# A third chunk projected from rows turned with both LayerNorm factors, a third pair of turned-row buffers, and a new order for the MLP and its two ends

## The chip, the cores and the metric

The kernel runs on one core of one Trainium2 chip. Its time is in device microseconds (us) for one execution; runs of the kernel before lie between 1086.4 and 1087.1 us.

## The reference, cut to what matters

One sequence of 2048 rows `x` with 448 columns, all float32. `xn` is the LayerNorm of `x`; the result is `x + attention(xn) + mlp(layernorm(xn))`.

```python
xn = layernorm(x)
# A: 16 query heads of 28, one shared key head and one shared value head
q = (xn @ wq) split into 16 heads; k = xn @ wk; v = xn @ wv
A = softmax(q k^T / sqrt(28)) v, heads joined, @ wo
# B: a second LayerNorm, then two dense layers (448 -> 1792 -> 448)
y = layernorm(xn)
B = gelu(y @ w1 + b1) @ w2 + b2
out = x + A + B
```

The second LayerNorm of an already normalised row differs from the first by one factor for each row. So every row has a first factor `lnr` (for the projections) and the product of both, `lnq` (for the MLP).

## The kernel before, in words

The rows are handled in four chunks, 0 to 3, of 512 rows (four tiles of 128). There are three stages, laid out in one program order by Python code; each engine works its own instructions strictly in that order.

**Projections (about 0 to 65 us).** For chunk c there are four `q_slot`s (c, 0) to (c, 3), each of eleven matmuls on TensorE (PE) that project the chunk on 128 of 512 columns of wk, wv and wq; a factor of float32 precision is got from a high and a low part (`xh`, `xl`; `wah`, `wal`). While chunk c is projected, chunk c+1 is made ready (`norm_parts`, L273): `center` (L280) scales and shifts a tile on ScalarE (ACT, 448 columns, L288) and its last 64 columns once more on VectorE (DVE, L289); `turn` (L293) turns it by four PE transposes (L297), and ACT (L298) and DVE (L299) write it to `xh` and `xl`. The statistics of a chunk are DVE chains (`bn`, `bn_end`, `rstd`: L194 to L240) with one square root on ACT. The result of a q_slot is evacuated by `evac` (L385) during the next slot: ACT writes the high part (L389) and DVE the low part (L396), which leave by DMA. At (c, 0) ACT also writes `vt`, which PE turns (L410) two slots on and DVE copies (L411).

A chunk in `KEPT` (L35: 2 and 3) is turned once only, with `lnq`, and its turned rows stay for the MLP. Its projections need `lnr`: `unscale` (L248) spreads the ratio of the factors over the partitions with four float32 matmuls (L251) and an ACT copy `ib`, and every evac of this chunk starts with a DVE multiplication by `ib` (L388). A chunk that isn't kept (0 and 1) is turned a second time, with `lnq`, during the MLP. The dictionary `more`, filled by `later`, holds jobs (statistics, second factors, unscale) for the slot in which they are put in.

**MLP (about 65 to 471 us).** 56 slots n, one for each chunk in `MLP_ORDER` (2, 3, 0, 1) and each of 14 blocks ft of 128 hidden columns. Slot n holds the first layer of its block (`mlp1`, L636: eleven matmuls into the PSUM tile `ph`, then the GELU by ACT and GpSimd (POOL), in pieces `middle` and `ending`), and the second layer of the block of slot n-2 (`mlp2`, L662: twelve matmuls L673 from `hh`, `hl` and the weights `w2h`, `w2l`). The weights of the second layer are split by `w2_split` (L362: ACT `high` L367, then DVE and POOL `low` L371) for two blocks at a time. The dictionary `stages` of `slot` (L683) says after which of the twelve matmuls a piece is issued. Between these matmuls stand steps of two streams of the attention: `mxs` (scores whose maxima DVE takes, L561 and L562) and `tq` (scores of the heads that are turned by way of DRAM, L595, with DVE L596, ACT L613 and four DMAs). Their PSUM tiles `m` share three banks here.

**Attention (about 471 to 1085 us).** Scores L931, exponentials L932, the weighted sum L903, with the rest of `mxs` and `tq` between; what is left of `mxs` is shared out over the steps. Loads of this stage are issued from POOL (`loads = pool`, L949).

Of the kernel before, what the change touches and what calls it, by code (L numbers as in the profile page):

```python
# [16 lines left out]
P = 128  # L17
# [17 lines left out]
KEPT = 2, 3  # L35
MLP_ORDER = 2, 3, 0, 1
# [5 lines left out]
def block_kernel(ctx, tc, x, wq, wk, wv, wo, w1, b1, w2, b2, out):  # L42
# [11 lines left out]
    xt_p = ctx.enter_context(tc.tile_pool(name="xt", bufs=2))  # L54
# [18 lines left out]
    xl_p = ph1.enter_context(tc.tile_pool(name="xl", bufs=2))  # L73
# [120 lines left out]
    def rstd(dst, var, n, norms):  # L194
        m = len(norms)
        v = tmp.tile([P, 3, m, n], F32, name=f"rs{m}{n}", bufs=2)
# [20 lines left out]
    def bn_end(c, k0=0, n=CT):  # L217
# [10 lines left out]
        if c in KEPT:  # L228
            ratio = ratios[c] = tmp.tile([P, CT], F32, name="ratio", bufs=2)
            dve.tensor_mul(ratio, at[:, 1], lnq[:, ts])  # L230
# [42 lines left out]
    def norm_parts(c, second, first=False, bank=mtile):  # L273
        second = second or c in KEPT
# [5 lines left out]
        def center(k):  # L280
# [3 lines left out]
            else:  # L284
                xn = tmp.tile([P, 4 * P], F32, name="xn", bufs=2)
# [3 lines left out]
            dve.tensor_scalar(xn[:, D:512], src[:, 384:448], scale[:, t:t + 1], bias[:, t:t + 1],  # L289
                              op0=ALU.mult, op1=ALU.add)  # L290
# [12 lines left out]
    def norm_first(bank):  # L303
        center, turn = norm_parts(0, False, True, bank)
        ends = seconds
# [122 lines left out]
    seconds = [bn_end(0, 0, 2), bn_end(0, 2, 2)]  # L428
    norm_first(qbank)
    seconds.append(stats(1))  # L430
# [5 lines left out]
    for c, at in ((2, ((0, 1), (0, 2), (0, 2), (0, 3))), (3, ((1, 0), (1, 1), (1, 2), (1, 3)))):  # L436
# [6 lines left out]
        later(c - 1 if c == 2 else c, 3 if c == 2 else 0, lambda c=c: unscale(c), c == 3)  # L443
    for g, at in zip((seconds[0], seconds[1], seconds[2]), ((2, 2), (2, 2), (1, 0))):
        later(*at, lambda g=g: next(g))
    for g in seconds[0:2]:
        later(2, 3, lambda g=g: next(g))
    later(2, 3, lambda: act.activation(warm, one, AF.Tanh))
# [28 lines left out]
    for c in range(NCH):  # L477
        if c + 1 < NCH:
            center, turn = norm_parts(c + 1, False, bank=lambda shape: (qbank, mtile)[next(turns) % 2](shape))
        for i in range(4):  # L480
# [23 lines left out]
            for part, k in (("", "c0 c1", "t0 c2 t1 c3", "t2 t3") if c == 0 else  # L504
# [131 lines left out]
    def mlp1(c, ft):  # L636
# [5 lines left out]
        hz = hrp.tile([P, CW], F32, name="hz", bufs=2)  # L642
        act.activation(hx, ph, AF.Identity, bias=b1t[:, ft:ft + 1])  # L643
# [18 lines left out]
    def mlp2(c, ft, stages):  # L662
# [20 lines left out]
    def slot(n):  # L683
# [330 lines left out]
```

## Time and profile before

| | |
|---|---|
| median of 3 runs | 1086.64 us (1086.4 to 1087.1) |
| profiled execution | 1086.84 us |
| its span | 1085.1 us |
| granted TensorE clock | 0.999 |
| PE busy | 1072.9 us |
| DVE busy | 907.4 us |
| ACT busy | 726.8 us |
| POOL busy | 562.0 us |

The span is the time from the first to the last instruction of the profiled execution. A busy PE does not mean a PE at its peak: matmuls are pipelined and each record is longer than the distance to the next one, so what a step costs on PE is read from the distance between the starts of records. In a timeline a row has its start, its length, the engine, the line, the operation and the tiles; a bracket gives how long the engine sat idle before it and what ended that.

### The profile page before, as it was taken

To read this page: it belongs to the slowest core of one execution; us is meant where nothing else is said; L and a number is where in the kernel's file an instruction comes from. 1 tells how busy PE (TensorE), PEld (TensorE's weight loads), DVE (VectorE), ACT (ScalarE), POOL (GpSimd) and SP (SyncE) were. 2 spreads that over 40 slices of the span, in tenths; PEclk is the share of its full clock that TensorE was granted. 3 is DMA by queue.
4 is the path that set the end of the run, shared out by engine and by line. 5 is a ranking of instruction groups with operands and counts; after the bars stand their busy time and mean duration, and the time that the engine had idled before them with its cause. 6 is when DMAs were issued, how large, how long until landed. Compare 5 with 4: busy or idle time off the path is not lost.

```text
span 1085.1 us, 17677 instructions
## 1 busy us (share of the span) xinstructions
PE 1072.9 (99%) x5889; PEld 721.6 (67%) x5889; DVE 907.4 (84%) x1846; ACT 726.8 (67%) x1262; POOL 562.0 (52%) x694
## 2 busy tenths in 40 slices
PE   9989999999999999999999999999999999999998
PEld 8768888888888888865555556555556555555455
DVE  6789899898988998877999997899997889886744
ACT  6665556666666666559777776677775777765784
POOL 5359897778777877854333433433442343243220
PEclk9999999999999999999999999999999999999999
DMA  8774456777877777776977798588796778885820
GB/s 268 251 213 140 121 142 170 195 179 179 214 187 180 184 196 192 210 163 152 201 187 185 179 219 206 145 196 190 184 212 172 177 174 199 201 200 131 186 53 34
DMA packets 140102, 194.45 MB, mean 179 GB/s; under 512 B 17078, under 2 KB 95596, under 8 KB 140012
## 3 DMA queue, kind: packets, MB, share of 16 engines
q1 hardware_dynamic: 127276, 171.43, 62.8%
q0 software_dynamic: 11328, 21.33, 8.5%
q8 instruction: 46, 0.75, 0.3%
q10 hardware_dynamic: 1408, 0.57, 0.2%
q14 instruction: 44, 0.36, 0.1%
HBM read 114.30 MB, written 77.71 MB: 177 GB/s over the span
## 4 chain that ended last, share of the span: by engine, by line
PE 90%; DMA 4%; DVE 3%; issue 1%; POOL 1%; ACT 1%; SPq 0%; DVEq 0%; POOLq 0%; ACTq 0%
PE po L903 21%; PE m L561 18%; PE m L931 17%; PE m L673 12%; PE ph L182 10%; PE m L595 5%; DMA raw<-in_B_w_dram 1%; PE m L793 1%; PE m L794 1%; PE m L795 1%; PE ph L185 1%; PE ph L187 1%; PE po L886 1%; PE m L886 1%; DMA a<-in_A_x_dram 1%
## 5 line engine op out<-in xcount | busy, mean ns | idle before, releaser
L562 DVE TENSOR_REDUCE mx<-m 128x1 f32<-128x512 f32 x784 | 506.5, 679 | 78.2 <-PE m L561 68.4
L932 ACT ACTIVATE p<-m 128x512 f32<-128x512 f32 x784 | 402.6, 609 | 161.4 <-PE m L931 161.2
L561 PE MATMUL m<-ks,qm 128*128 128x512 f32 x784 | 321.4, 410 | 0.7 <-DVE mx L562 0.6
L931 PE MATMUL m<-xh,ks 128*128 128x512 f32 x784 | 257.3, 397 | 0.1
L903 PE MATMUL po<-p,vs 128*32 128x512 f32 x1920 | 230.8, 598 | 0.0
L561 PEld LDWEIGHTS m<-ks,qm 128*128 128x128 f32 x784 | 147.0, 187 | 116.8 <-ACT p L932 37.0
L596 DVE TENSOR_SCALAR_CACHE_REDUCE raw<-m 128x512 f32<-128x512 f32 x240 | 161.6, 689 | 17.4 <-PE m L595 10.6
L931 PEld LDWEIGHTS m<-xh,ks 128*128 128x128 f32 x784 | 146.1, 188 | 42.1 <-issue 5.8
L914 DVE STREAM_TRANSPOSE p<-half 128x1024 f32<-128x1024 f32 x120 | 148.2, 1236 | 5.3 <-PE m L886 2.0
L613 ACT ACTIVATE raw<-raw,m 128x1024 f32<-128x1024 f32 x120 | 133.0, 1150 | 2.0 <-DVE m L602 2.0
L903 PEld LDWEIGHTS po<-p,vs 128*32 128x32 f32 x1920 | 50.1, 109 | 113.4 <-issue 108.4
L643 ACT ACTIVATE hx<-ph,b1t 128x512 f32<-128x512 f32 x55 | 37.9, 690 | 124.2 <-PE ph L187 120.2
L595 PE MATMUL m<-ks,q 128*128 128x512 f32 x240 | 94.6, 394 | 1.7 <-DVE raw L596 1.7
L658 POOL TENSOR_TENSOR hl<-hx,hh 128x512 fp32r<-128x512 f32 x56 | 72.5, 1295 | 33.2 <-ACT hh L656 33.2
L673 PE MATMUL m<-w2h,hl 128*128 128x448 f32 x224 | 82.1, 368 | 1.4 <-POOL hl L658 1.4
L673 PE MATMUL m<-w2l,hh 128*128 128x448 f32 x224 | 81.4, 365 | 0.6 <-DVE w2l L371 0.6
L673 PE MATMUL m<-w2h,hh 128*128 128x448 f32 x224 | 81.3, 364 | 0.2 <-DMA td<-raw 0.2
L646 POOL TENSOR_TENSOR hz<-hz,hx 128x512 f32<-128x512 f32 x56 | 72.8, 1300 | 4.7
L548 POOL DMA_DIRECT2D xh<-mn x15 | 8.2, 545 | 129.2 <-ACT mn L544 129.2
L651 POOL TENSOR_TENSOR hx<-hx,hz 128x512 f32<-128x512 f32 x56 | 72.4, 1293 | 4.7
L182 PE MATMUL ph<-xh,w1h 128*128 128x512 f32 x165 | 65.0, 394 | 0.0
L182 PE MATMUL ph<-xh,w1l 128*128 128x512 f32 x165 | 64.5, 391 | 0.0
(182 smaller groups left out, 1384.0 us busy)
## 6 DMA issues: line engine op xcount, KB each, us to landing
td<-raw SPq DMA_DIRECT2D x240, 256.0 KB
half<-td SPq DMA_DIRECT2D x120, 512.0 KB
xh<-qd POOLq DMA_DIRECT2D x60, 168.0 KB, 4.2
a<-in_A_x_dram SPq DMA_DIRECT2D x28, 224.0 KB
qm<-qd POOLq DMA_DIRECT2D x112, 56.0 KB, 4.2
qd<-qe SPq DMA_DIRECT2D x24, 256.0 KB
qm<-qd SPq DMA_DIRECT2D x84, 56.0 KB
ad<-a SPq DMA_DIRECT2D x16, 224.0 KB
```

What stands on the lines that cost most here:

```text
L182: pe.matmul(ps, w, v, start=(n == 0), stop=False)
L561: pe.matmul(pm, qm[:, t * P:(t + 1) * P], ks[:, n * CW:(n + 1) * CW], start=True, stop=True)
L562: dve.tensor_reduce(mx[:, CT * j + t, n:n + 1], pm, axis=AX.X, op=ALU.max)
L595: pe.matmul(sc, q3[i][:, t * P:(t + 1) * P], ks[:, n * CW:(n + 1) * CW], start=True, stop=True)
L596: dve.tensor_scalar(raw[:, :, 4 * n:4 * n + 4, :].rearrange("p r b i -> p b r i"), sc.rearrange("p (b r i) -> p b r i", r=4, i=32), SCALE, ...
L613: act.activation(raw[:, rs], raw[:, rs], AF.Exp, bias=m3[:, 4:5], scale=1.0)
L646: pool.tensor_mul(hz, hz, hx)
L673: pe.matmul(m2[k], h[:, k * P:(k + 1) * P], w[:, ft, :], start=(ft == 0 and i == 0), stop=(ft == NF - 1 and i == 2))
L903: pe.matmul(po[32 * j:32 * j + 32, :], vs[:, kt, :], ps.pop((u, kt, j)), start=(kt == 0), stop=(kt == NT - 1))
L914: dve.transpose(p.rearrange("p k (g j) -> p g k j", j=32), halves[u, kt // 8][:, :, 32 * (kt % 8):32 * (kt % 8) + 64].rearrange("p g (k j) ...
L931: pe.matmul(s, ks[:, kt * P:(kt + 1) * P], qss[u][:, j, :], start=True, stop=True)
L932: act.activation(p, s, AF.Exp, scale=SCALE)
```

## The change

- `KEPT` becomes 1, 2, 3: chunk 1 too is turned once, with `lnq`, its q_slots are multiplied by `ib`, and its second turn falls away. `MLP_ORDER` becomes 1, 2, 3, 0.
- `xt_p` and `xl_p` get three buffers instead of two. For the space, the DMA scratch in SBUF is set to 2048 bytes a partition (`dynamic_dma_scratch_size`, not given before), the `xn` tiles are one of `tmp` and one of `wqp`, and the four-wide `rs` tile has one buffer.
- The second factors of chunk 0 are one four-wide chain (`second_of_first`) at slots (3, 0) and (3, 1) instead of two two-wide ones at (2, 2) and (2, 3). The tails of chunk 2's `center` go from DVE to ACT. `unscale` stands at (c, 0) for each kept chunk. The evac of the last q_slot starts one piece earlier.
- At the start of the MLP, the three extra `mxs` steps of slot 2 are gone, and the first `w2_split` and the `middle` of slots 0 and 1 are issued earlier.
- At its end, the `ending` of slot 54 is issued ahead of the GELU of slot 55, the b2 additions of the last chunk five slots earlier, and the last `mlp2` takes its matmuls in pairs of row tiles.

```diff
-KEPT = 2, 3
-MLP_ORDER = 2, 3, 0, 1
+KEPT = 1, 2, 3
+MLP_ORDER = 1, 2, 3, 0
...
-    xt_p = ctx.enter_context(tc.tile_pool(name="xt", bufs=2))
+    xt_p = ctx.enter_context(tc.tile_pool(name="xt", bufs=len(KEPT)))
...
-    xl_p = ph1.enter_context(tc.tile_pool(name="xl", bufs=2))
+    xl_p = ph1.enter_context(tc.tile_pool(name="xl", bufs=len(KEPT)))
...
-        else:
-            r = rstd(lnrq[:, 1:2, ts], lnp[:, ts, 1], n, (True,))
-            next(r)
-            yield
-            next(r)
-            shift(True, ts)
+        yield
+
+    def second_of_first():
+        ts = slice(0, CT)
+        r = rstd(lnrq[:, 1:2, ts], lnp[:, ts, 1], CT, (True,))
+        next(r)
+        yield
+        next(r)
+        shift(True, ts)
         yield
...
-                xn = tmp.tile([P, 4 * P], F32, name="xn", bufs=2)
+                xn = (wqp if k % 2 and not again else tmp).tile([P, 4 * P], F32, name="xn", bufs=1)
...
-            dve.tensor_scalar(xn[:, D:512], src[:, 384:448], scale[:, t:t + 1], bias[:, t:t + 1],
-                              op0=ALU.mult, op1=ALU.add)
+            if c == 2:
+                act.activation(xn[:, D:512], src[:, 384:448], AF.Identity, bias=bias[:, t:t + 1], scale=scale[:, t:t + 1])
+            else:
+                dve.tensor_scalar(xn[:, D:512], src[:, 384:448], scale[:, t:t + 1], bias[:, t:t + 1],
+                                  op0=ALU.mult, op1=ALU.add)
...
-        later(c - 1 if c == 2 else c, 3 if c == 2 else 0, lambda c=c: unscale(c), c == 3)
...
+    for c in KEPT:
+        later(c, 0, lambda c=c: unscale(c), True)
+    later(0, 3, later_one)
+    g = second_of_first()
+    for k in (0, 1):
+        later(3, k, lambda g=g: next(g))
+    later(3, 1, lambda: act.activation(warm, one, AF.Tanh))
...
+            if (c, i) == (NCH - 1, 3):
+                _, end = evac()
             if low is not None:
                 low()
...
-    evac()[1]()
+    end()
...
-    def mlp1(c, ft):
+    def mlp1(c, ft, before):
...
+        before()
         act.activation(hx, ph, AF.Identity, bias=b1t[:, ft:ft + 1])
...
+        if (c, ft) == (NCH - 1, NF - 1):
+            order.sort(key=lambda e: (e[0] // 2, e[1]))
...
-            if split(*mslots[n]):
+            if split(*mslots[n]) and n > 1:
                 high, low = w2_split(n // 2)
-                if n > 1:
-                    high()
-            middle, ending = yield from mlp1(*mslots[n])
-        if n == 2:
-            for _ in range(3):
-                maxed += mxs.step()
-            later_low()
+                high()
+            before = none
+            if n == len(mslots) - 1:
+                before, closing = closing, none
+            middle, ending = yield from mlp1(*mslots[n], before)
...
+        if n == 0:
+            high, later_low = w2_split(0)
+            stages = {0: texp, 1: middle, 2: texp, 3: high}
         if n == 1:
-            stages, later_low = {0: closing, 1: high, 5: middle}, low
+            stages = {0: closing, 1: later_low, 2: middle}
...
-        if 9 < ft:
-            line(CT * MLP_ORDER[c] + ft - 10)
-            if ft > 10:
-                a = lines[CT * MLP_ORDER[c] + ft - 11]
-                pool.tensor_add(a, a, b2b)
+        k = ft - (10 if c < NCH - 1 else 5)
+        if c < NCH and 0 <= k < CT:
+            line(CT * MLP_ORDER[c] + k)
+        if c < NCH and 0 < k <= CT:
+            a = lines[CT * MLP_ORDER[c] + k - 1]
+            pool.tensor_add(a, a, b2b)
...
-    nc = _bacc.Bacc("TRN2", target_bir_lowering=False, num_devices=1)
+    nc = _bacc.Bacc("TRN2", target_bir_lowering=False, num_devices=1, dynamic_dma_scratch_size=2048)
```

More of the change, by code (lines that the diff above doesn't have):

```diff
@@ L273, in norm_parts @@
     def norm_parts(c, second, first=False, bank=mtile):
-        second = second or c in KEPT
+        again, second = second, second or c in KEPT
         xh = xt_p.tile([P, 4, CW], F32R, name="xh")
@@ L304, in norm_first @@
         center, turn = norm_parts(0, False, True, bank)
-        ends = seconds
+        ends = [bn_end(0, 0, 2), bn_end(0, 2, 2)]
         bn(0)
@@ L427, in block_kernel @@
     idle = mtile([P, P])
[L428 removed]
     norm_first(qbank)
[L430 removed]
+    g = stats(1)
+    later_one = lambda g=g: next(g)
     more = {}
```

11 lines of the change are left out of this document (3 added, 8 removed).

## The prediction

> **What bounds the kernel now.** I read the page first, then who PE waited for, then the timelines of the two places where it waits. All times are us.
>
> ```profile
> span 1085.1 us, 17677 instructions
> PE 1072.9 (99%) x5889; PEld 721.6 (67%) x5889; DVE 907.4 (84%) x1846; ACT 726.8 (67%) x1262; POOL 562.0 (52%) x694
> ```
> ```profile
> PE m L595 <- DVE raw L596: 1.7, 2, 1.3
> PE m L673 <- POOL hl L658: 1.4, 2, 0.7
> PE qp L182 <- DVE xl L299: 0.7, 2, 0.4
> PE m L410 <- ACT vt L393: 0.7, 1, 0.7
> PE m L673 <- DVE w2l L371: 0.6, 1, 0.6
> ```
>
> PE is the bound in all three stages: 99% of the span, and its listed waits are small (total, times, longest). So there are two ways to gain: less work on PE, and the waits above. All of these stand in the projections, the first MLP slots and the last two. DVE and ACT are not far behind: all but one of these waits are for them, and in the projections their chain decides when PE may go on. The reader is to see how little there is to win: 5.1 for the five together.
>
> **The change part by part.** *The second turn of chunk 1.* These are the starts of three MLP slots; the first holds a turn, the second none.
>
> ```profile
> 210.28 0.40 PE L182 MATMUL ph<-xh,w1h 128*128 128x512 f32 x1
> ...
> 217.90 0.40 PE L182 MATMUL ph<-xh,w1h 128*128 128x512 f32 x1
> ...
> 224.95 0.40 PE L182 MATMUL ph<-xh,w1h 128*128 128x512 f32 x1
> ```
>
> 7.62 against 7.05: a turn costs PE 0.57, so four that fall away give **-2.3**. Their four ACT and DVE pieces ran beside PE in these slots and give nothing more. The chunk's `lines` loads and the reordered SP queue go with them; PE waited for no load in these slots.
>
> The b2 additions of the last chunk, and their line loads on SP, only move a few slots ahead; POOL is busy 52% of the span, and without that cover each would hold its queue for less than the 1.61 of POOL's longest subtraction below.
>
> *One more unscale.* From its first matmul to the second one of the next q_slot, less one normal distance:
>
> ```profile
> 38.93 1.05 PE L251 MATMUL m<-ident,ratio 128*128 128x128 f32 x8
> ...
> 40.06 0.39 PE L182 MATMUL qp<-xl,wah 128*128 128x512 f32 x1
> 40.29 0.39 PE L182 MATMUL qp<-xh,wal 128*128 128x512 f32 x1
> ```
>
> 40.06 - 38.93 - 0.23 = **0.9** of PE, if PE is what sets the pace there. It is not:
>
> *The evacuation chain of chunks 1 and 2.* With a factor, an evac is DVE (L388), then ACT (L389), then DVE (L396), one behind the other, where before ACT and DVE of chunk 1 had one hand-over less. These are DVE's rows, then one of ACT and one of PE.
>
> ```profile
> 29.95 0.16 DVE L246 SCALAR_TENSOR_TENSOR lnqb<-lnp,lnrq 128x4 f32<-128x4 f32 x1
> ...
> 35.99 0.14 DVE L230 TENSOR_TENSOR ratio<-rs,lnrq 128x4 f32<-128x4 f32 x1
> ...
> 36.25 0.62 DVE L215 BATCH_NORM_STATS2 st<-hh 128x6 f32<-128x448 f32 x1
> 36.79 0.27 DVE L411 COPY vs<-m 128x128 f32<-128x128 f32 x1
> ...
> 38.61 0.68 DVE L299 TENSOR_TENSOR xl<-m,xh 128x512 fp32r<-128x512 f32 x1
> ...
> 42.61 0.16 DVE L246 SCALAR_TENSOR_TENSOR lnqb<-lnp,lnrq 128x4 f32<-128x4 f32 x1
> ...
> 49.65 0.69 DVE L388 TENSOR_TENSOR qp<-qp,ib 128x512 f32<-128x512 f32 x1
> 51.01 0.69 DVE L396 TENSOR_TENSOR qe<-qp,qe 128x512 fp32r<-128x512 f32 x1 [0.66 <-DMA qd<-qe]
> ...
> 52.21 0.68 DVE L299 TENSOR_TENSOR xl<-m,xh 128x512 fp32r<-128x512 f32 x1
> ```
> ```profile
> 50.37 0.60 ACT L389 ACTIVATE qe<-qp 128x512 fp32r<-128x512 f32 x1 [1.62 <-DVE qp L388]
> ```
> ```profile
> 52.95 0.50 PE L182 MATMUL qp<-xl,wah 128*128 128x512 f32 x1 [0.40 <-DVE xl L299]
> ```
>
> Chunk 2 already runs with factors, and serves as the pattern: from the end of its `lnqb` row (42.77) to the end of the last L299 (52.89) it takes 10.1, and PE then waits 0.40 for it. Chunk 1 gets the same sequence, with one more L215 (36.79 - 36.25 = 0.54) in it; its start moves from 30.11 to 30.4, for the two ratio operations (36.25 - 35.99 = 0.26) now stand ahead. 30.4 + 10.1 + 0.54 = 41.05 is when (2, 0) gets its last `xl`; its second matmul stood at 40.06 before, with one unscale ahead as well. So PE is 1.0 late here.
>
> Then the statistics of chunk 3: from the last L299 (end 39.29) to `lnqb` (42.77) they took 3.5. Into this stretch come the evac of (1, 2), which takes 1.36 from L388 to L396, the L388 of (1, 3) with 0.69, and some 0.2 for the square root on ACT, queued behind the copy of (1, 3): 41.05 + 3.5 + 2.25 = 46.8, and the pattern again, 56.9. PE's (3, 0) goes on there instead of at 52.95: **3.9 late**, 0.9 of it its own unscale.
>
> The tails that go from DVE to ACT I cost at nothing: ACT waited 1.62 for DVE within this pattern. They cost at most 0.6 each (the 512-column copy of 50.37) and two stand ahead of the first copy, so 1.2 if that cover were gone; the DVE operations they replace could give back as much. The third buffers remove no wait, since PE and ACT waited for no turned-row buffer in the rows above.
>
> *Chunk 3's slots and the second factors.*
>
> ```profile
> 54.30 0.69 DVE L396 TENSOR_TENSOR qe<-qp,qe 128x512 fp32r<-128x512 f32 x1 [0.67 <-ACT qe L389]
> ...
> 55.43 1.44 DVE L204 SCALAR_TENSOR_TENSOR rs<-rs 128x2 f32<-128x2 f32 x1
> ...
> 57.92 0.16 DVE L204 SCALAR_TENSOR_TENSOR rs<-rs 128x2 f32<-128x2 f32 x1
> ...
> 58.58 0.69 DVE L388 TENSOR_TENSOR qp<-qp,ib 128x512 f32<-128x512 f32 x1
> ...
> 68.77 0.69 DVE L396 TENSOR_TENSOR qe<-qp,qe 128x512 fp32r<-128x512 f32 x1 [0.71 <-ACT qe L389]
> ```
> ```profile
> 55.24 1.61 POOL L354 TENSOR_TENSOR w1l<-raw,w1h 128x672 fp32r<-128x672 f32 x1 [6.24 <-issue]
> ```
> ```profile
> 70.11 0.50 PE L595 MATMUL m<-ks,q 128*128 128x512 f32 x1 [1.33 <-DVE raw L596]
> ```
>
> Between 54.99 and 58.58 DVE did both two-wide chains, 3.6, of which 1.3 (1.44 against 0.16) is the stretched L204 beside a POOL subtraction. This stretch goes. One four-wide chain comes back behind the evac of (3, 0): half of the undisturbed rest is 1.1, with the same stretching 2.4. I take 2.4, because it stands behind a weight split for POOL again, and because the copy of `vt` behind it must wait for PE in any case. The Trainium skill, SBUF — State Buffer, section SBUF: two separate sides, says that a DVE operation with two SBUF inputs and a GpSimd operation that reads SBUF lock one another out of a shared port pair for the whole instruction; the rows of 55.24 and 55.43 agree. By this rule the chain is again 2.4, without it 1.1, which moves the sum by 0.3 at most.
>
> The new order of the last two evacs lets the L388 of (3, 3) run while ACT copies: -0.6. So the first L596 moves from 69.4 by +3.9 - 3.6 + 2.4 - 0.6 = +2.1, and the L595 that waits for its bank from 70.11 to 72.2: **+2.1** in all. The waits for `vt` (0.7) and for L596 (1.3) are within this number: they are swallowed by the later start, not won.
>
> *The first MLP slots.*
>
> ```profile
> 77.31 1.00 PE L561 MATMUL m<-ks,qm 128*128 128x512 f32 x3
> 78.53 0.44 PE L673 MATMUL m<-w2h,hh 128*128 128x448 f32 x1 [0.23 <-DMA td<-raw]
> ...
> 80.67 0.67 PE L673 MATMUL m<-w2l,hh 128*128 128x448 f32 x2 [0.61 <-DVE w2l L371]
> ```
>
> The three extra L561 (3 x 0.23) leave this place: -0.7. They come back in the attention, where PE is busy throughout: **+0.7**. With `high` and `low` earlier, the gap ahead of 78.53 (1.22 - 0.7 = 0.5) and the one ahead of 80.67 (0.6, and 0.1 to get going) go. What is late next: `high` now stands behind two exponentials on ACT, and the subtraction L371 on DVE waits for it; queued behind it are slot 2's L596, which hold the three `m` banks that PE needs. I put 0.2 to 0.8 on that, and take 0.5. Slots 0 to 2 together: -0.7 - 0.5 - 0.7 + 0.5 = **-1.4**.
>
> *The last slots.*
>
> ```profile
> 459.13 0.69 ACT L643 ACTIVATE hx<-ph,b1t 128x512 f32<-128x512 f32 x1 [2.65 <-PE ph L187]
> ...
> 465.73 0.63 ACT L656 ACTIVATE hh<-hx 128x512 fp32r<-128x512 f32 x1 [2.58 <-POOL hx L651]
> ```
> ```profile
> 463.77 0.47 PE L673 MATMUL m<-w2h,hl 128*128 128x448 f32 x1 [0.74 <-POOL hl L658]
> ...
> 468.09 0.47 PE L673 MATMUL m<-w2h,hl 128*128 128x448 f32 x1 [0.69 <-POOL hl L658]
> ```
>
> The two waits with their restarts (0.1 each) are 1.6. With slot 54's `ending` first, its `hl` is there in time, and the first goes. But `hx` of slot 55 then starts some 0.7 later than 459.13. Its `hh`, which ended at 466.4, ends at 466.7, since ACT has idle time ahead of it, while PE now arrives 0.8 earlier, near 466. So PE waits 0.7 for `hh` and, with the matmuls in pairs, some 0.2 for `hl`: 1.6 becomes 0.9, **-0.7**. Bounds: nothing, and all 1.6.
>
> *The small DMA scratch.*
>
> ```profile
> q0 software_dynamic: 11328, 21.33, 8.5%
> ```
> ```profile
> qm<-qd POOLq DMA_DIRECT2D x112, 56.0 KB, 4.2
> ```
>
> Only POOL's queue can feel it. 11328 packets in the attention's 614 us on 16 engines, each 4.2 under way, are about 5 at a time for an engine. I cost it at nothing. By the Trainium skill, DMA: Bandwidth & Descriptors, sections Terms and SWDGE vs HWDGE vs iDMA, a descriptor has 16 bytes and GpSimd writes them to rings in an SBUF carveout: an estimate of 128 places from 2 KB, well over 5, but no run here shows the ring's limit.
>
> **Sum:** -2.3 + 2.1 - 1.4 + 0.7 - 0.7 = -1.6. The profiled 1086.84 becomes 1085.2 and the median 1086.64 becomes **1085.0**.
>
> **The rivals.** *The chain stays hidden.* If ACT and DVE keep pace (the hand-overs overlap better than in chunk 2's pattern), PE pays the unscale only and the listed waits go: -2.3 + 0.9 - 0.7 - 1.3 - 0.2 for restarts - 1.2 (the two gaps) - 0.7 = -5.5, **1081.1**. For it: DVE's added L388 are partly paid by tails that leave it. Against it: PE waited 0.40 for this very chain with one chunk fewer.
>
> *The chain isn't caught up* (slower). If chunk 3's slots don't win back the 1.8, because the four-wide chain is stretched and the copy of `vt` waits for PE behind it, L595 comes 3.9 late, and with L371 holding the banks the gaps of slot 2 return (1.2): -1.6 + 1.8 + 1.2 = +1.4, **1088.0**. It decides once L595 comes after 73.8 (72.2 + 1.6). For it: every link is serial. Against it: 3.6 of DVE work leaves that place.
>
> *The ring is too small* (slower). If POOL must wait for free places, the loads of `qm` in the attention (28 of four) come late; 0.5 each is +14, **1099**. It decides below some 5 places for an engine. Nothing speaks for it but that it is untried.
>
> That the second turn stays is excluded: the four groups of L297 are missing from the changed program's order of instructions.
>
> **How the numbers follow.** Forecast 0.60 (1085.0, its own range 1083.0 to 1086.9), hidden chain 0.21, not caught up 0.15, ring 0.04. The range of 8 in 10 reaches from 1081.7 to 1087.5. About 0.2%, 2.2, is what a measurement of this kernel can tell from no change: below 1084.5 lie the hidden chain and a third of the forecast, together 0.42; above 1088.8 the ring and a fifth of the second rival, with 0.08; within, 0.50.
>
> **What would show it.** Right: in the projections PE's waits for L299 grow, to about 1.0 ahead of (2, 0) and 1.0 ahead of (3, 0); the last L595 of slot 0 starts near 72; slot 2's second layer has no wait for L371; slots with a turn are four instead of eight; one wait near 0.9 is left in the last two slots, for `hh`. Wrong: the first MLP matmul at about 65.4 as before (hidden chain), or POOL DMAs longer than before, with PE waiting for `qm`.

## The result and the profile after

The changed kernel takes **1088.58 us** (median; runs from 1087.68 to 1091.58), the kernel before 1086.64 (1085.93 to 1087.91): ratio 1.0022, 95% interval 1.0015 to 1.0028. The forecast was 1085.0, with 1087.5 as the upper end. Two things are to be explained: where the gain went, and why the runs now lie four microseconds apart instead of two. The profiled execution is one of the shortest, 1087.7, so its trace shows only 0.9 of the 1.9.

From the page of the changed kernel, the span and PE's busy time, and below that, what PE waited for (in total, times, longest):

```profile
span 1085.9 us, 17626 instructions
...
PE 1072.8 (99%) x5881; PEld 719.8 (66%) x5881; DVE 906.6 (83%) x1833; ACT 723.4 (67%) x1258; POOL 560.7 (52%) x694
```
```profile
PE m L604 <- DVE raw L605: 2.1, 3, 1.0
PE qp L182 <- DVE xl L305: 1.4, 3, 0.5
...
PE m L685 <- ACT hh L666: 0.7, 1, 0.7
PE m L685 <- POOL hl L668: 0.7, 1, 0.7
...
PE m L900 <- ACT p L946: 0.6, 1, 0.6
```

Lines have moved by up to 14: L595 is now L604, L596 L605, L371 L377, L299 L305, L561 L570, L673 L685. PE has 16 matmuls fewer for turns, 8 more for the third `unscale`, and the same busy time. The old waits for `vt`, `w2l` and `mx` are gone; others have come. The timeline of PE shows where, with the second turn gone as forecast (the starts of the same three MLP slots as in the prediction):

```profile
40.76 0.50 PE L182 MATMUL qp<-xh,wah 128*128 128x512 f32 x1 [0.23 <-ACT xh L304]
...
41.71 0.50 PE L182 MATMUL qp<-xl,wah 128*128 128x512 f32 x1 [0.44 <-DVE xl L305]
...
57.57 0.50 PE L182 MATMUL qp<-xl,wah 128*128 128x512 f32 x1 [0.44 <-DVE xl L305]
...
73.31 0.50 PE L604 MATMUL m<-ks,q 128*128 128x512 f32 x1 [0.67 <-DVE raw L605]
...
80.94 0.50 PE L604 MATMUL m<-ks,q 128*128 128x512 f32 x1 [0.98 <-DVE raw L605]
...
90.39 0.47 PE L685 MATMUL m<-w2h,hl 128*128 128x448 f32 x1 [0.66 <-POOL hl L668]
...
213.28 0.40 PE L182 MATMUL ph<-xh,w1h 128*128 128x512 f32 x1
...
220.31 0.40 PE L182 MATMUL ph<-xh,w1h 128*128 128x512 f32 x1
...
227.34 0.40 PE L182 MATMUL ph<-xh,w1h 128*128 128x512 f32 x1
...
437.55 0.50 PE L604 MATMUL m<-ks,q 128*128 128x512 f32 x1 [0.42 <-DVE raw L605]
...
467.42 0.67 PE L685 MATMUL m<-w2h,hh 128*128 128x448 f32 x2 [0.73 <-ACT hh L666]
...
1045.56 0.64 PE L900 MATMUL m<-p,vs 128*32 128x256 f32 x8 [0.58 <-ACT p L946]
```

The reader is to follow the distance to the kernel before: 73.31 against 70.11 is 3.2 late, 213.28 against 210.28 still 3.0; the slot that had a turn (to 220.31) gives 0.59 back, and the four together 2.4.

For the variants below I measure two stretches, both between the starts of L185, the matmul ahead of a slot's last first-layer matmul: **the start**, from slot 0's to slot 5's, and **slot 52**, from slot 51's to slot 52's. In the changed kernel they are 103.46 - 72.03 = 31.43 and 437.88 - 430.15 = 7.73; in the kernel before 100.47 - 68.17 = 32.30 and 437.19 - 429.49 = 7.70.

### The profile page after: what moved, and what is told of

Same layout as the page of the kernel before. It is cut to its first block, busy times and chain, and to the rows that moved or that the text cites. A ratio compares the mean times of both kernels' runs of the same rounds, so it can differ in the third digit from the quotient of the medians.

```text
span 1085.9 us, 17626 instructions
## 1 busy us (share of the span) xinstructions
PE 1072.8 (99%) x5881; PEld 719.8 (66%) x5881; DVE 906.6 (83%) x1833; ACT 723.4 (67%) x1258; POOL 560.7 (52%) x694
## 4 chain that ended last, share of the span: by engine, by line
PE 90%; DVE 4%; ACT 2%; POOL 2%; DMA 2%; issue 1%; SPq 0%; ACTq 0%; DVEq 0%; POOLq 0%
PE po L917 20%; PE m L570 18%; PE m L945 17%; PE m L685 12%; PE ph L182 10%; PE m L604 5%; PE m L807 1%; PE m L808 1%; PE m L809 1%; PE ph L187 1%; PE ph L185 1%; DMA qd<-qe 1%; PE qp L182 1%; PE po L900 1%; DVE xl L305 1%
## 5 line engine op out<-in xcount | busy, mean ns | idle before, releaser
L570 PE MATMUL m<-ks,qm 128*128 128x512 f32 x784 | 321.4, 410 | 0.1
L570 PEld LDWEIGHTS m<-ks,qm 128*128 128x128 f32 x784 | 147.0, 187 | 114.8 <-ACT p L946 41.6
L605 DVE TENSOR_SCALAR_CACHE_REDUCE raw<-m 128x512 f32<-128x512 f32 x240 | 162.5, 690 | 18.9 <-PE m L604 10.8
L604 PE MATMUL m<-ks,q 128*128 128x512 f32 x240 | 94.7, 395 | 2.1 <-DVE raw L605 2.1
L685 PE MATMUL m<-w2h,hl 128*128 128x448 f32 x224 | 81.4, 366 | 0.7 <-POOL hl L668 0.7
L685 PE MATMUL m<-w2h,hh 128*128 128x448 f32 x224 | 81.0, 364 | 0.7 <-ACT hh L666 0.7
L685 PE MATMUL m<-w2l,hh 128*128 128x448 f32 x224 | 81.3, 364 | 0.0
L476 POOL DMA_DIRECT2D qm<-qd x112 | 57.4, 519 | 29.5 <-PE m L945 23.3
```

The costliest lines, as they stand in the source:

```text
L570: pe.matmul(pm, qm[:, t * P:(t + 1) * P], ks[:, n * CW:(n + 1) * CW], start=True, stop=True)
L604: pe.matmul(sc, q3[i][:, t * P:(t + 1) * P], ks[:, n * CW:(n + 1) * CW], start=True, stop=True)
L605: dve.tensor_scalar(raw[:, :, 4 * n:4 * n + 4, :].rearrange("p r b i -> p b r i"), sc.rearrange("p (b r i) -> p b r i", r=4, i=32), SCALE, ...
L685: pe.matmul(m2[k], h[:, k * P:(k + 1) * P], w[:, ft, :], start=(ft == 0 and i == 0), stop=(ft == NF - 1 and i == 2))
```

## The experiments

Theory after the first comparison: the third kept chunk itself costs about what it gives, and the new order of the MLP's ends loses, at three places, what it was forecast to win. Rivals: the small scratch; the tails on ACT; a chain that is late as a whole. Each ratio below is against runs of the kernel before that were taken beside the variant.

**The scratch alone.**

```diff
-    nc = _bacc.Bacc("TRN2", target_bir_lowering=False, num_devices=1)
+    nc = _bacc.Bacc("TRN2", target_bir_lowering=False, num_devices=1, dynamic_dma_scratch_size=2048)
```

> The kernel before with one thing of the change alone, the DMA scratch of 2 KB. Theory A (the loss comes from PE's waits at three places, and the scratch costs nothing): the same as the kernel before, 1086.6 give or take 0.4, and the highest of its runs no more than about 1 above the lowest. Rival B (the small scratch makes GpSimd's DMAs late in some runs, which is why the changed kernel's runs reach 1091.6): a median of 1087.5 or more, and single runs above 1089.

Measured: 1086.94, ratio 1.0002 (0.9993 to 1.0010), the highest run 1088.63. The rival falls: the scratch costs nothing that shows in the median. The runs lie 2.5 apart where theory A had about 1; without that one run it is 1.3. The estimate of 128 places in the prediction, from the Trainium skill, DMA: Bandwidth & Descriptors, sections Terms and SWDGE vs HWDGE vs iDMA, is not contradicted, though where the ring ends no run here shows.

**Chunk 2's tails back on DVE.**

```diff
-            if c == 2:
-                act.activation(xn[:, D:512], ...)
-            else:
-                dve.tensor_scalar(xn[:, D:512], ...)
+            dve.tensor_scalar(xn[:, D:512], ...)
```

> The changed kernel with chunk 2's tails back on DVE. Theory A1 (the two tails of 0.33 each ahead of ACT's first copy of chunk 1 make the chain late, the bound of 1.2 in the prediction): the first L395 behind the tails starts some 0.6 earlier than 32.81, PE's second wait ahead of (2, 0), 0.44, shrinks to nothing, and 0.3 to 0.7 of it lasts to the first MLP slot: 1087.9 to 1088.3 against 1088.6. Rival A2 (DVE is the slower one in this stretch, so its four added operations of about 0.23 eat what ACT wins): no change, or 0.3 slower.

Measured: 1090.10, ratio 1.0026 (1.0015 to 1.0036). In its timeline of PE both waits ahead of (2, 0) stay:

```profile
40.95 0.50 PE L182 MATMUL qp<-xh,wah 128*128 128x512 f32 x1 [0.49 <-ACT xh L301]
...
41.90 0.50 PE L182 MATMUL qp<-xl,wah 128*128 128x512 f32 x1 [0.44 <-DVE xl L302]
```

ACT's first copy of chunk 1 behind the tails starts at 33.01, not 0.6 ahead of 32.81, and the first MLP matmul at 69.49 against 69.31. So A1 fell, and at this place A2 holds: it doesn't matter which of the two engines has the tails. The time is 1.5 above the changed kernel's median where A2 had at most 0.3, with intervals that overlap; in its profile the excess is at two stretches that the edit doesn't touch, 33.17 and 8.18.

**Slots 0 to 2 in the old order.**

```diff
...
+        if n == 2:
+            for _ in range(3):
+                maxed += mxs.step()
+            later_low()
...
-        if n == 0:
-            high, later_low = w2_split(0)
-            stages = {0: texp, 1: middle, 2: texp, 3: high}
         if n == 1:
-            stages = {0: closing, 1: later_low, 2: middle}
+            stages, later_low = {0: closing, 1: high, 5: middle}, low
```

> The changed kernel with the work of MLP slots 0 to 2 in the order of the kernel before: the three score matmuls back in slot 2, w2's split and the gelu pieces at their old places. Theory A (the new order buys two waits and shifts the banks of the attention's end): the waits of 0.98, 0.66 and 0.58 go, with their restarts 2.5; the old gaps ahead of w2h and w2l return, 1.2; so -1.3, 1087.3. Rival C (the old order now suffers as much because the chain ahead of it is late): 1088.6 or more.

Measured: 1087.63, ratio 1.0008 (1.0000 to 1.0017), about 1 below the changed kernel. The waits of 0.98, 0.66 and 0.58 are gone; the start takes 31.61, slot 52 takes 8.43. Theory A holds, with 1.0 for the forecast 1.3.

**The ring of banks shifted.**

```diff
-    ring = itertools.cycle([mp] * 3 + [mp3] * 3 + [mp1])
+    ring = itertools.chain([mp] * 3, itertools.cycle([mp] * 3 + [mp3] * 3 + [mp1]))
```

> The changed kernel with the attention's ring of seven PSUM banks started three tiles later, so that the last unit meets the banks as in the kernel before; no instruction is added, taken or moved. Theory A (the new wait of 0.58 for p at 1045.56 is a wait for a bank, since three more tiles go through the ring in the attention): the wait goes, -0.8, 1087.8. Rival D (the wait is for ACT's pace in the last unit): it stays where it is, 1088.6.

Measured: 1089.01, ratio 1.0021 (1.0012 to 1.0031). The wait at 1045 went, so it is one for a bank; but two waits for `p`, of 0.7 and 0.2, came at the attention's first steps, and the sum is nothing. This profiled execution was a long one (1091.11), with a start of 105.63 - 71.45 = 34.18 and a slot 52 of 441.27 - 432.29 = 8.98, and it shows where long executions differ. First the changed kernel's DVE and ACT at the start, then this one's:

```profile
75.20 2.55 DVE L571 TENSOR_REDUCE mx<-m 128x1 f32<-128x512 f32 x4
79.65 0.62 DVE L377 TENSOR_TENSOR w2l<-raw,w2h 128x448 fp32r<-128x448 f32 x1 [1.90 <-ACT w2h L373]
80.19 0.69 DVE L605 TENSOR_SCALAR_CACHE_REDUCE raw<-m 128x512 f32<-128x512 f32 x1
```
```profile
78.61 0.95 ACT L373 ACTIVATE w2h<-raw 128x896 fp32r<-128x896 f32 x1 [0.58 <-ACT raw L622]
```
```profile
80.29 0.95 ACT L373 ACTIVATE w2h<-raw 128x896 fp32r<-128x896 f32 x1 [2.14 <-DMA qd<-qe]
```
```profile
81.33 0.62 DVE L377 TENSOR_TENSOR w2l<-raw,w2h 128x448 fp32r<-128x448 f32 x1 [2.91 <-DMA td<-raw]
81.87 0.68 DVE L605 TENSOR_SCALAR_CACHE_REDUCE raw<-m 128x512 f32<-128x512 f32 x1
```

DVE stands idle for 1.90 and 2.91 with a subtraction at the head of its queue that waits for ACT's copy, while the score matmuls of slot 2, which need nothing of either, hold PE's banks behind it. (The last row names a DMA; the copy, which ended at 81.24, came later.) ACT's copy itself waits for the stores of `qe`: `w2h` stands where the pool of `qe` stood, and the program makes its first writer wait for that pool's stores. These are the last eight in SP's queue, 0.6 each. They were all issued by 75.51 in the changed kernel's profile and by 77.10 here:

```profile
70.83 4.68 SPq L409 DMA_DIRECT2D qd<-qe  x8
```
```profile
72.42 4.68 SPq L409 DMA_DIRECT2D qd<-qe  x8
```

The copy starts 3.1 and 3.2 behind that (the 0.58 ahead of it in the changed kernel isn't ACT's either, whose exponential ended at 78.04). SP itself had stood 2.0 behind one DMA before, in this execution:

```profile
SPq L409 <- DMA raw<-in_B_w_dram: 2.0, 1, 2.0
```

So a delay in SP's queue ahead of these stores now reaches PE. It reaches PE at one more place, which isn't the new order's: the L604 that waits at 74.01 here (1.94) names DVE, but the first L605 had freed the bank at 72.66. What is late is most likely the load of `ks` for this matmul, which SP had issued by 70.78 in the changed kernel and by 72.38 here; that the matmul can wait for this load three later variants show (`ks<-qe`, 0.27 to 0.97).

A third thing lengthens this start. Behind the second wait PE's clock falls; the same matmul takes longer:

```profile
82.62 0.50 PE L604 MATMUL m<-ks,q 128*128 128x512 f32 x1 [1.98 <-DMA td<-raw]
...
84.66 0.63 PE L570 MATMUL m<-ks,qm 128*128 128x512 f32 x1
...
87.30 0.39 PE L570 MATMUL m<-ks,qm 128*128 128x512 f32 x1
```

The granted clock (1.00 is full speed) was 0.50 from 83.8 to 87.2 here, and for as long in the two runs below that move w2's copy, in both at a wait of 2.43. It stayed at 1.00 there in the changed kernel's own profile (wait 0.98) and in three variants with waits of 1.86 to 2.13, so the length of this one wait alone doesn't decide it. It costs less than it looks, for a later wait of 0.66 for `hl` is then gone: from slot 2's L185 to slot 4's these three take 15.29 to 15.64, the four others 15.15 to 15.17. So the 2.75 by which this start is longer than 31.43 are 1.25 at the first wait, 1.0 at the second and 0.5 behind it. Of the changed kernel's 21 runs, five of the seven longest have a mean granted clock of 0.998; the fourteen others have 0.999 or more.

**The q load ahead of the addition, w2's split later, and all three together.** In slot 8 of the last chunk `load_q(0)` is issued ahead of the line load and the b2 addition; or w2's copy moves to slot 1; or both, with the ring moved on in another way:

```diff
+        if (c, ft) == (NCH - 1, 8):
+            load_q(0)
         k = ft - (10 if c < NCH - 1 else 5)
...
```
```diff
...
-            stages = {0: texp, 1: middle, 2: texp, 3: high}
+            stages = {0: texp, 1: middle, 2: texp}
         if n == 1:
-            stages = {0: closing, 1: later_low, 2: middle}
+            stages = {0: closing, 1: later_high, 2: middle, 3: later_low}
```
```diff
+    ring = itertools.chain(([mp] * 3 + [mp3] * 3) * 4, itertools.cycle([mp] * 3 + [mp3] * 3 + [mp1]))
```

> The changed kernel with one call moved: in slot 8 of the last chunk the zeroing of xh on GpSimd and xh's loads on SP are issued ahead of the b2 addition and the line load. Theory E (the b2 addition of 1.16, now ahead of the zeroing, holds SP's queue, so the store of a turned row behind it leaves 2.7 later, and DVE's L605, which needs that row's buffer, starts late by as much as the store is slow): PE's wait at 437.55, 0.42 in the profiled run of the changed kernel and 0.88 to 1.67 in three others, goes; 1087.6 to 1088.1, and fewer runs above 1089. Rival F (the wait comes from the b2 additions' load on GpSimd in general): it stays, 1088.6.

> The changed kernel with w2's first split one slot later: ACT's copy behind slot 0's hh, DVE's and GpSimd's subtraction behind the four L605 of slot 1; all else stays. Theory G (the copy is the first to write where wqp's tiles stood, and waits until the last stores of qe land, at 78.6 in the profiled run of the changed kernel and at 80.3 in the run with the shifted ring; DVE's subtraction waits for the copy, the four L605 stand behind it, and PE waits for their bank, 0.98 to 2.08): PE's wait at 80.94 goes, some 0.5 returns ahead of the first second-layer matmul, since the copy now ends behind 81; 1087.4 to 1088.0, and the highest run below 1090.5. Rival H (the four L605 are late because the whole chain is): the wait stays, 1088.6.

> The two edits of the runs with the earlier q load and the later w2 split together, and the ring of banks moved on by four places in another way than before: the bank of mp1 is left out in the first four laps of the attention. Theory (three separate waits, 0.4 to 1.7 at 437, 1.0 to 2.0 at 81, 0.8 at 1045): they add up, 1086.2 to 1087.0, about the kernel before, with runs no more than 2 apart. Rival (what one wait gives up, the next takes): 1087.5 or more.

Measured: 1088.76, 1.0018 (1.0009 to 1.0027); 1089.44, 1.0025 (1.0014 to 1.0036); 1088.83, 1.0022 (1.0013 to 1.0032). All three missed. In the second, ACT's copy no longer waits for a DMA, as G said, but L377 still stands ahead of the four L605, which belong to slot 2 and not, as I had read it, to slot 1. With the copy later the wait only grows, here to 2.4, with the half clock behind it. ACT, DVE and PE's total there:

```profile
79.37 0.93 ACT L373 ACTIVATE w2h<-raw 128x896 fp32r<-128x896 f32 x1
```
```profile
80.39 1.06 DVE L377 TENSOR_TENSOR w2l<-raw,w2h 128x448 fp32r<-128x448 f32 x1 [2.92 <-ACT w2h L373]
```
```profile
PE m L604 <- DVE raw L605: 3.8, 3, 2.4
```

In the first, slot 52 takes 8.21. SP's queue in the kernel before, in the changed one and in this one:

```profile
425.11 1.65 SPq L530 DMA_DIRECT2D xh<-qd  x4
426.87 3.58 SPq L616 DMA_DIRECT2D td<-raw  x4
```
```profile
426.88 2.59 SPq L539 DMA_DIRECT2D xh<-qd  x4
429.58 3.75 SPq L625 DMA_DIRECT2D td<-raw  x4
```
```profile
427.07 2.55 SPq L539 DMA_DIRECT2D xh<-qd  x4
429.67 0.38 SPq L274 DMA_DIRECT2D a<-in_A_x_dram  x1
430.15 3.46 SPq L625 DMA_DIRECT2D td<-raw  x4
```

The store of a turned row, `td<-raw`, leaves 2.7 later in the changed kernel, 0.7 of which is the whole's delay, and the new order puts the line load in front instead. In the third, `p`'s wait moved from the attention's end to its start again (0.8).

**The last slots alone**, on the kernel before (slot 54's `ending` ahead of slot 55's GELU, pairs in the last `mlp2`, line loads and additions five slots earlier, the q load ahead of them):

```diff
...
+            if n == len(mslots) - 1:
+                before, closing = closing, none
...
-        if 9 < ft:
-            line(CT * MLP_ORDER[c] + ft - 10)
+        k = ft - (10 if c < NCH - 1 else 5)
+        if c < NCH and 0 <= k < CT:
+            line(CT * MLP_ORDER[c] + k)
...
```

> The kernel before with the change of the last two MLP slots alone (slot 54's ending ahead of slot 55's hx, the last second layer in pairs, the last chunk's b2 additions and line loads earlier), with xh's zeroing and loads ahead of the b2 addition of slot 8. The prediction's -0.7, and the -0.65 that the two traces show between slot 55 and the attention: 1086.2 beside 1086.9. Rival (without the third kept chunk the last slots gain nothing, or the addition delays hl as before): 1086.9.

Measured: 1087.43, ratio 1.0007 (0.9998 to 1.0016), not 1086.2. From slot 55 to the attention it gains 0.6, as forecast, but slot 52 takes 438.24 - 429.71 = 8.53, 0.8 more than in the kernel before. So the moved loads lose 0.8 in this profile without any third kept chunk.

**The subtraction behind the scores; the line loads at 9 to 12; both mended; w1's last split late.**

```diff
...
         if n == 1:
-            stages = {0: closing, 1: later_low, 2: middle}
+            stages = {0: closing, 1: later_high, 2: middle}
...
             middle, ending = yield from mlp1(*mslots[n], before)
+        if n == 2:
+            later_low()
```
```diff
-        k = ft - (10 if c < NCH - 1 else 5)
+        k = ft - (10 if c < NCH - 1 else 9)
```
```diff
-                w1_split(n)
+                if n < 7:
+                    w1_split(n)
...
     end()
+    w1_split(7)
```

> The changed kernel with both halves of w2's first split moved: ACT's copy one slot later as in the run before, and the subtractions L377 behind the four score matmuls and L605 of slot 2, where the kernel before has them. Theory G2 (it is L377 in front of the four L605 that makes PE wait: DVE stands idle for ACT's copy while PE's three banks wait for DVE; where the copy comes, and whether it waits for a DMA, only sets how long): from slot 0's last first-layer matmul to slot 5's takes 30.9 to 31.2, where the kernel before took 32.30, the changed one 31.43 in its own profile and 32.40 to 34.18 in five others; time 1087.0 to 1087.6, the runs about 2 apart. Rival H (DVE is simply late from the chain ahead): 32 or more, 1088.5.

> The changed kernel with the last chunk's line loads in slots 9 to 12 and the b2 additions in slots 10 to 13, in place of 5 to 8 and 6 to 9. Theory E2 (whatever of the two stands ahead of slot 8's xh loads and the turned row's store, the zeroing behind an addition or the store behind a load of 224 KB, makes the store late; the earlier q load cleared the one and put the other in its place): slot 52 falls from 7.73 to 8.98 in the looks so far to 7.4 to 7.7, as in the kernel before; 1087.6 to 1088.0. Rival (the store is late because the start made everything late): slot 52 stays above 8.

> The edits of the two other runs of this call together, and the three score matmuls back in slot 2 as well, so that the attention's ring of banks meets its end as in the kernel before. If the three places are what the change lost: the chain's 3.9 at the start of the MLP, less 0.7 and 1.2 in the first slots, less 2.4 for the turns, less 0.65 in the last slots: about 1.0 below the kernel before, 1085.6 to 1086.2, ratio 0.9985 to 0.9995. If the chain alone eats the gain: 1087 or more.

> The same with w1's last split issued behind the last evac: ACT's copy of 0.94, which stands between the two last copies of qe (70.00 and 71.33 in the changed kernel), then comes after both. Theory (that copy is the rest of the late start: the first L605 at 72.56 where the prediction had 71.5): the first L605 0.6 to 0.9 earlier behind the first MLP matmul than in the run beside it, PE's wait for its bank, 0.67, gone; 0.5 to 0.8 less than that run. Rival (DVE's two L402, or PE itself, set the start): no difference.

Measured: 1087.58, 1.0010 (1.0001 to 1.0019); 1088.04, 1.0014 (1.0005 to 1.0023); 1086.78, 1.0005 (0.9996 to 1.0014); 1086.68, 1.0004 (0.9995 to 1.0013). With the subtraction behind the scores the start takes 102.10 - 71.29 = 30.81, and PE waits there for `w2l` instead of a bank:

```profile
PE m L604 <- DVE raw L605: 1.2, 2, 0.6
...
PE m L685 <- DVE w2l L377: 0.8, 1, 0.8
```

G2 holds for the wait: DVE works the four L605 first, and the wait for the bank is gone with the copy of ACT as late as before. That profiled execution is the shortest of its eleven runs (1086.54), and these reach 1090.0, 3.5 apart where G2 had 2. With the loads at 9 to 12 slot 52 takes 438.78 - 431.75 = 7.03, below the 7.4 to 7.7 of E2; the runs below show how much of that lasts. Mended at both places the kernel is level with the one before, not 1.0 below: with the additions later, PE waits 1.1 for `hh` near the end instead of 0.7, slot 53 takes 0.3 more, and the start, 31.20, wins 0.4 less than with the subtraction alone. With w1's split late PE's wait for its first bank falls from 0.97 to 0.27, as its theory had it; but the wait for `w2l` grows from 0.4 to 0.7, and the start is 31.12, so that here its rival is as near. In each of these last two kernels one run of eleven lies above 1090 (1090.07 and 1090.78, mean granted clock 0.997 and 0.998), so the subtraction's place is not all of the spread.

**The third kept chunk alone**, that is the changed kernel with the two ends of the MLP (slots 0 to 2 as in the third run above, last slots, line loads, additions) taken back:

```diff
...
-            if n == len(mslots) - 1:
-                before, closing = closing, none
...
-        k = ft - (10 if c < NCH - 1 else 5)
...
+        if 9 < ft:
+            line(CT * MLP_ORDER[c] + ft - 10)
...
```

> The kernel before with the third kept chunk alone: chunk 1's factors, the third buffers, the 2 KB scratch, the tails on ACT, the order 1, 2, 3, 0 of the MLP, the chunk 0 factors later and the last two evacs reordered; MLP slots 0 to 2, the last slots, line loads and b2 additions as before. Theory K (the chain eats what the turns give): first MLP matmul 3.8 later, 0.7 of it won back at the wait for L605, 2.4 at the turns: about 0.7 above the kernel before, 1087.2 to 1087.6. Rival L (the chain is caught up as predicted and the new order of the MLP's ends spoils the rest): -2.3 and +2.1 less the wait, 1085.6 to 1086.4.

Measured: 1086.87, ratio 1.0002 (0.9993 to 1.0011), the runs 1.0 apart. What PE waited for in the MLP is as in the kernel before:

```profile
PE m L682 <- POOL hl L667: 1.4, 2, 0.7
...
PE m L604 <- DVE raw L605: 0.7, 1, 0.7
...
PE m L682 <- DVE w2l L377: 0.6, 1, 0.6
```

It lies between the two theories: the first MLP matmul is 3.5 late, the wait for L605 gives 0.7 back and the turns 2.4, which leaves 0.4; slot 52 was 0.3 shorter, which lies within the spread of that place (table below). So the chunk is worth nothing that shows here, and it is the ends that made the kernel slower: the interval of the changed kernel begins at 1.0015, above this one's 1.0011.

**What is left as a gain, on the kernel before**: the reordered last evacs with w1's last split behind them; the same with the new order of the last two slots; and that with the line loads at 9 to 12:

```diff
-                w1_split(n)
+                if n < 7:
+                    w1_split(n)
...
+            if (c, i) == (NCH - 1, 3):
+                _, end = evac()
...
-    evac()[1]()
+    end()
+    w1_split(7)
```
```diff
...
+        if (c, ft) == (NCH - 1, NF - 1):
+            order.sort(key=lambda e: (e[0] // 2, e[1]))
...
+            if n == len(mslots) - 1:
+                before, closing = closing, none
...
```
```diff
-        if 9 < ft:
-            line(CT * MLP_ORDER[c] + ft - 10)
...
+        k = ft - (10 if c < NCH - 1 else 9)
+        if c < NCH and 0 <= k < CT:
+            line(CT * MLP_ORDER[c] + k)
...
```

> The kernel before with the last two evacs in the changed kernel's order and w1's last split behind them, nothing else. Theory (two links of the chain leave the path to the first L596: DVE's L388 overlaps ACT's copy, and ACT's copy of 0.94 no longer stands between the two copies of qe): PE's wait of 1.33 for its bank falls to 0.0 to 0.7 and the time by 0.6 to 1.3, 1085.4 to 1086.0. Rival (what PE gains there it waits at w2's split, which then meets its stores earlier): 1086.6.

> The same with the new order of the last two slots (slot 54's ending first, second layer in pairs), the line loads and b2 additions at their old places. Theory: another 0.3 to 0.65 off, since one of the two waits for hl goes; the additions in slots 11 to 13 still hold GpSimd ahead of hl: 1084.9 to 1085.6. Rival (an addition of 1.16 ahead of the last hl takes all of it): as the run beside it.

> The same again with the line loads one slot earlier than before (9 to 12) and the additions in 10 to 13, clear of slot 8's store and of the very last slot. Theory: slot 52, 7.70 in the kernel before and 7.03 in the changed kernel with the same place of the loads, gains up to 0.7: 1084.4 to 1085.4. Rival (the 7.03 was chance of the store's landing): as the run beside it.

Measured: **1085.55**, 0.9989 (0.9980 to 0.9998); **1085.28**, 0.9988 (0.9979 to 0.9997); 1085.90, 0.9993 (0.9985 to 1.0002). The first two lie below both kernels, by about 0.1% and with upper ends just under 1. In the first, ACT copies `qe` twice in a row where w1's copy stood between, and PE's wait of 1.33 is 0.45:

```profile
66.11 1.20 ACT L389 ACTIVATE qe<-qp 128x512 fp32r<-128x512 f32 x2 [1.41 <-DVE qp L388]
67.20 0.94 ACT L353 ACTIVATE w1h<-pair 128x896 fp32r<-128x896 f32 x1
```
```profile
69.23 0.47 PE L599 MATMUL m<-ks,q 128*128 128x512 f32 x1 [0.45 <-DMA ks<-qe]
```

The second doesn't stand clear of the first, and its theory isn't borne out at its place: from slot 55's L185 to the first weighted sum it takes 20.80 where the first takes 20.72, for PE now waits 1.06 for `hh` and 0.36 for `hl` in place of the two waits of 0.7 for `hl`. That stretch takes 20.13 to 20.17 in the seven profiles with the new order, the additions in slots 6 to 9 and the ring as it was, and 20.47 to 20.52 in the four with the additions in 10 to 13. So the new order needs the early additions for its 0.6, and these lose 0.8 in slot 52. Moving the loads to 9 to 12 gives nothing: the 7.03 above was the better end of a spread.

The two stretches in all profiles, by what each kernel has at that place:

| start (slot 0 to 5) | us |
|---|---|
| kernel before, scratch alone, last slots alone | 32.30, 32.24, 32.29 |
| the same order, w1's last split late | 31.08, 30.84, 30.89 |
| third kept chunk, old order | 31.61, 31.60 |
| changed order | 31.43, 33.17, 34.18, 32.40, 32.73 |
| changed order, copy later | 33.26, 33.34 |
| subtraction behind the scores; with the three score matmuls in slot 2 | 30.81; 31.20, 31.12 |

| slot 52, line loads in slots | us |
|---|---|
| 10 to 13, as before | 7.70, 7.44, 7.36, 7.30, 7.34 |
| 5 to 8, as changed | 7.73, 8.18, 8.43, 8.98, 8.21, 8.04, 8.34, 8.53, 7.83 |
| 9 to 12 | 7.03, 7.67, 7.52, 7.49 |

The changed kernel's own profile holds the shortest value of its row in both tables. That is why its trace shows so little of the loss. Three of the values include the half clock: 34.18, 33.26 and 33.34. Three of the slot 52 values, 8.21, 8.34 and 8.53, have the q load moved ahead as well.

## Why the prediction was wrong, point by point

Four terms of the sum failed. The first is **"The first MLP slots", -1.4**, and in it the price of the new wait, "0.2 to 0.8 ... and take 0.5". The place was named rightly (L371 waits for `high`, slot 2's L596 are queued behind it and hold PE's banks), its size wasn't: 0.98 in the changed kernel's own profile and 1.9 to 2.1 in the variants that leave this order alone. I priced it by ACT's two exponentials, which end at 78.04, and didn't ask what else the copy waits for: the stores of the pool that it writes over. The wait of 0.66 for `hl` at 90.39 comes on top. From the L604 that waits for its bank to slot 5 the changed kernel won 0.2 (30.15 against 30.36) in its own profile, and lost 0.7 to 1.3 in those variants (105.63 - 74.01 = 31.62 in the one with the shifted ring, 0.5 of it behind the half clock). With the old order of these slots back the ratio fell from 1.0022 to 1.0008.

Second, **the chain, +2.1**: the L595 came 3.2 late. Of the 1.1 by which it was too small, 0.7 stands in the chain itself: the second matmuls of (2, 0) and (3, 0) start at 41.71 and 57.57 where 41.05 and 56.9 were forecast, so that (3, 0) goes on 4.6 late and not 3.9. Why, the runs leave open; the tails back on DVE didn't win it. The rest is in the catching up, 1.4 for the forecast 1.8 (the first MLP matmul stands at 69.31 against 65.45). The -0.6 for the reordered evacs didn't come, since ACT's copy of w1 stood between the two copies, as the runs with this copy last show. Turns and chain together were forecast at -0.2; the changed kernel's profile has +0.8, and the chunk alone a ratio of 1.0002.

Third, **the b2 additions and line loads, cost at nothing**. The sentence weighed POOL's and SP's time, not what is behind them: the addition holds the zeroing of `xh`, that SP's loads, these the store of a turned row, and its buffer DVE. By the table's means, 8.25 against 7.43, it is 0.8. The place could be seen beforehand: the prediction puts all five waits in the projections, the first MLP slots and the last two, but 0.40 of the wait for L596 stands in slot 52 of the kernel before:

```profile
436.86 0.50 PE L595 MATMUL m<-ks,q 128*128 128x512 f32 x1 [0.40 <-DVE raw L596]
```

Fourth, **the three L561 back in the attention, +0.7**: they cost 0.4 there (PE is 0.08 late at 490, 0.44 at 1030), but three tiles more turn the ring of seven banks, so that the last unit's `m` meets a bank with a fresher `p`: 0.8 more.

What held:
- The turns: -2.3 forecast, -2.4 measured.
- That DVE and ACT, not PE, set the pace in chunks 1 and 2: PE waits for `xl` at 41.71 and 57.57.
- The four-wide chain came stretched, as taken. These are DVE's and POOL's rows of the changed kernel at the four-wide chain; the rule of the Trainium skill, SBUF — State Buffer, section SBUF: two separate sides, agrees with them:

```profile
64.67 1.41 DVE L204 SCALAR_TENSOR_TENSOR rs<-rs 128x4 f32<-128x4 f32 x1
```
```profile
64.41 1.65 POOL L360 TENSOR_TENSOR w1l<-pair,w1h 128x672 fp32r<-128x672 f32 x1 [2.03 <-ACT w1h L359]
```

- The last slots: -0.7 forecast; PE is 0.69 late at slot 55 and 0.09 at the first weighted sum (479.24 against 479.15), with one wait of 0.73 for `hh` left.
- The scratch: nothing.

So -1.6 becomes, in the profiled execution, -2.4 for the turns, +3.2 for the chain, -0.2 for the first slots, -0.6 for the last, +0.4 and +0.8 in the attention: +1.2 at PE's last matmul (1081.84 against 1080.63). The span grew by 0.8; the rest is in the last stores. Here the first slots and the chain are off by about the same, 1.2 and 1.1. The longest profile adds 2.7 at the start (34.18) and 1.2 in slot 52 (8.98); the longest run of the changed kernel is 3.9 above its shortest.

Of the rivals, "the chain isn't caught up" came nearest, with 1088.0 and the same two mechanisms, the late L595 and L371 on the banks; it had been given 0.15. The point from which it was to decide, 73.8, was passed in some profiles (74.15, 74.01, where the first L605 had freed the bank by 73.42 and 72.66) and not in others (73.31), with the bank's wait in slot 2 in all of them. The shares of "chain" and "new order" that I had joined in it are separate: the first costs, with the turns, nothing on balance, the second is the loss.

Open remains what makes SP's queue slower in some executions; the traces show single DMAs that land late, not why. Open too is from which wait on the clock falls. How much of the spread each place carries was read from profiles, not tried one by one. The difference between variants of about 1 is near what their intervals can tell; firmer are the ratios of the changed kernel and of the chunk alone, whose intervals don't meet. The two kernels below the one before clear 1 by 0.0002 and 0.0003, and are the best of sixteen variants.

## What to carry to other kernels

Before an instruction is moved ahead in an in-order queue, list everything that it waits for, the release of the memory that it writes over included, and what behind it another engine is waiting for: a subtraction that nobody needed yet stopped four that held PE's banks. A load or an addition "with room to spare" is priced by what stands behind it in its queue, not by its engine's load. And when runs of a kernel spread more than they did, one trace shows one end of the spread: the profiles of variants that leave a place alone are samples of that place.

## What the runs showed of the hardware

SP's queue took 0.6 for each of the last stores of `qe`, 256 KB each (eight in 4.68 in the kernel before, the changed one and the one with the shifted ring), and the copy that waits for the last of eight started 3.1 and 3.2 after the last issue in the two executions compared: it was the issue that came 1.6 later, not the transfer that took longer. A rotation of PSUM buffers is a part of the schedule: three tiles more, or the ring's order, moved a wait of 0.6 to 0.9 between the two ends of a stage 614 long and hardly changed the sum. The granted clock of TensorE fell to 0.50 for about 3.4 behind waits of 1.98 and 2.43 in three executions, and not behind waits of 1.86 to 2.13 in three others; over the two slots that followed PE took 0.1 to 0.5 longer.
